# Global keys of batch 0 by short matmuls from the picked rows

## The chip, the cores and the metric

The kernel runs on one core of one Trainium2 chip. The metric is the time of the whole kernel on the device in microseconds (us). Measurements of one kernel are taken several times and the median is compared. TensorE is called PE in the profile, VectorE DVE, ScalarE ACT, GpSimd POOL and SyncE SP.

## The reference

Attention over 8 batches, 8 heads, 576 tokens and head size 64, followed by a two-layer feed-forward with squared ReLU (512 to 2048 to 512). Attention is local: a query sees the keys within 32 positions. Eight token indices, given at run time, are global: a global query sees every key, and every query sees the eight global keys.

```python
mask = np.abs(pos[:, None] - pos[None, :]) <= window
mask = mask | is_global[:, None] | is_global[None, :]
scores = np.where(mask, scores, -1000000000.0)
attn = np.exp(scores - max) / (sum + 1e-09)
x = (attn @ v) with heads side by side          # [4608, 512]
h = x @ w_in;  r = max(h, 0);  out = (r * r) @ w_out
```

## The kernel before, in words

**Layout.** A batch's 576 keys are cut into five tiles of 120 (the last 96). Each tile has 128 rows: rows 0 to 7 hold the eight global keys, the others the tile's own keys. The queries are laid out as 608 columns, four groups of 152: 144 tokens, then the eight global queries. A batch is worked in two halves of 304 columns. For each half a list of windows (WIN, or WIN2 without the two 8-column windows of the global queries) says which tile meets which columns. Since a window of columns often touches several tiles, a mask gives rows 0 to 7 a one only in the tile that owns a column, so that a global key counts once per query.

**Work on a head pair.** Heads go in pairs, four pairs per batch, numbered 0 to 3 in batch 0, 4 to 7 in batch 1 and so on. `scores` multiplies keys by queries into a PSUM bank pair ("sc" or "acc", by turns). `exps` is the exponential on ScalarE into `et`. `masked` multiplies by the mask on VectorE. `outputs` multiplies `et` by values for the numerators, and by ones for the denominators (in batches 0 and 1 by `one64` into a second bank, with the two heads of a pair on the two column halves of the array; L670). `finish_outputs` takes Ln and Exp of the negative on ScalarE for the reciprocal (L702, L703), sums the global queries' columns on VectorE (L709 in batch 0) and multiplies numerators by reciprocals into `xT` (L732), which is the input of the feed-forward. `global_outputs` normalizes the global queries. `scatter` (L751) then copies their eight columns to the run-time positions in `xT`, eight small copies on VectorE.

**Values of the global keys.** For batch 0 there is a one-hot matrix `oh` of the indices. `pick_values` multiplies it with the five value tiles (L449), VectorE casts the 8x512 result into `gv16` (L453), and `spread_values` (L457) copies it into rows 0 to 7 of each of the five value tiles, four copies on VectorE and one on ScalarE. Those rows had been set to zero by `clear_value_rows` (L441) at the start. For batch 1 the rows come from a fetch into `grow`, `gv16` is filled from there by ScalarE (L869) and spread in the same way. From batch 2 on, DMAs write the rows.

**Feed-forward.** It is cut into units. `mm1_half` (L543) is a pair of first-layer tiles for 256 tokens of chunk 0, eight units for the first 256 tokens and eight for the rest; `mm1` (L524) is one tile for 512 tokens of a later chunk; `mm2` (L587) is a quarter of the second layer for 128 tokens. The units wait in a Python list, and `take(n)` puts the next n into the instruction stream. Squares of the ReLU are on VectorE (L555), the ReLU mostly on ScalarE (L554).

**Order.** Nothing is scheduled automatically: every engine works through its instructions as written in the program. `SCHED` holds the counts: `g0`, `h0` to `h5`, `keep`, `b1` and `last` tell how many units are taken at which place, and the `w` entries how many filler matmuls of 512 columns on an idle tile `keep_warm` (L197) puts there; their results aren't used. In batch 0 the first halves of all four pairs are scored first (`half0`), then finished (`half0_out`, into "mm", "sc", "acc" and "mm" banks). `scatter(0, 0)` follows, then the first unit of chunk 0, then the second halves with units between. `scatter(0, 1)` comes ahead of the units for tokens from 256 on. There are three "mm" banks used in rotation and one "tr" bank.

**Queues.** Weights, batch 1's inputs and later values are fetched on GpSimd's queue in program order; three casts (L370) stand behind them, and then a one-element copy from `xT` (L909), which holds back the fetches for batch 2. Stores and transposing DMAs are on SP's queue.

Of the kernel before, what the change touches and what calls it, by code (L numbers as in the profile page):

```python
# [8 lines left out]
FP32 = mybir.dt.float32  # L9
# [3 lines left out]
AF = mybir.ActivationFunctionType  # L13
# [4 lines left out]
KT = 120  # L18
NT = 5
# [5 lines left out]
GTOK = 144  # L25
GRP = 152
NCOL = 608
BANKC = 304
# [11 lines left out]
)  # L40
W2 = 440
MB = (0, 456)
SCHED = dict(w8=2, w9=3, w5=3, w6=0, w7=4, wa=4, wb=3, wc=3, g0=1, w0=2, w1=4, w2=2, w3=2, w4=3, w=5, h0=0, h1=1, h4=1, h5=1, h2=1, h3=0, keep=1, b1=((3, 1, 3), (2, 1, 3), (2, 1, 3), (2, 1, 2)), last=((2, 1, 4), (3, 1, 4), (2, 1, 4), (2, 1, 7)))
ONES = 2.0**-7 * (1.0 + 15360.0 / 2**23)


# [1 line left out]
def kernel(  # L48
# [15 lines left out]
    P = 128  # L64
# [13 lines left out]
    def sbt(name, shape, dtype, bufs=1, tag=None):  # L78
        return sb.tile(shape, dtype, name=name, tag=(tag or name), bufs=bufs)
# [5 lines left out]
    def pst(tag, shape, dtype=FP32):  # L85
        return ps.tile(shape, dtype, name=tag, tag=tag, bufs=bufs_of[tag])
# [106 lines left out]
    def keep_warm(n):  # L193
        if n:
            w = pst("tr", [P, 512])
        for _ in range(n):
            nc.tensor.matmul(w, idle[:, 0:P], idle, start=True, stop=True)  # L197
# [245 lines left out]
            in_=idle[0:NG].rearrange("p (h d) -> p h d", d=D).unsqueeze(1).to_broadcast((NG, NT, H, D)),  # L443
        )

    def pick_values():
        gp = pst("mm", [P, 512])[0:NG]
        for x in range(NT):
            nc.tensor.matmul(  # L449
                gp.rearrange("p (h d) -> p h d", d=D), oh[:, x, :], vb[0][:, x, 0 : 2 * H : 2],  # L450
                start=(x == 0), stop=(x == NT - 1),
            )
        dve.tensor_copy(out=gv16, in_=gp.rearrange("p (h d) -> p h d", d=D))  # L453

    def spread_values(b, op, tiles=range(NT)):
        for x in tiles:
# [196 lines left out]
    lo, hi = slice(0, D), slice(D, P)  # L653
    PARTS = (((lo, 0, hi, 0), (hi, 1, lo, 1)), ((slice(0, P), 0, slice(0, P), 1),))

    def outputs(i, half, et, tag, wins, columns=False):
        b, hp = divmod(i, NHP)
        if tag == "mm":
            banks = [pst("mm", [P, 512]) for _ in range(2)]
        else:  # L660
            acc = pst(tag, [P, 2, 512])
            banks = [acc[:, x] for x in range(2)]
        vt = vb[b]
        vtf = vt.rearrange("p t x d -> p t (x d)")
        nw = len(wins[half])
        for n, (t, so, c0, w) in enumerate(wins[half] if columns else ()):
            o = c0 - half * BANKC
            for x in range(2):
                for e in range(2):
                    nc.tensor.matmul(  # L670
                        banks[x][D * e : D * e + D, o : o + w],
                        one64 if x else vt[:, t, 4 * hp + 2 * e], et[:, e, so : so + w],
                        start=(n == 0), stop=(n == nw - 1), skip_group_check=True,
                    )
        for e in () if columns else range(2):
            for n, (t, so, c0, w) in enumerate(wins[half]):
                o = c0 - half * BANKC
                vo = D * (4 * hp + e)
                nc.tensor.matmul(  # L679
                    banks[e][:, o : o + w], vtf[:, t, vo : vo + P], et[:, e, so : so + w],  # L680
                    start=(n == 0), stop=(n == nw - 1), skip_group_check=True,
                )
        return banks

    def global_outputs(b, gs, a, z, columns):
        gr = sbt("gr", [P, NHP, NG], FP32, bufs=2)
        if a == 0:
            gxs[b] = sbt("gx", [P, NHP, NG], FP16, bufs=2)
        for r, x, rs, xs in PARTS[columns]:
            dve.reciprocal(out=gr[r, a:z], in_=gs[rs, a:z, xs])  # L690
        for r, x, rs, xs in PARTS[columns]:
            dve.tensor_tensor(
                out=gxs[b][r, a:z], in0=gs[r, a:z, x], in1=gr[r, a:z], op=ALU.mult
            )

    def finish_outputs(i, half, acc, columns=False):
        b, hp = divmod(i, NHP)
        parts = PARTS[columns]
        av = [a[:, 0:BANKC].rearrange("p (k c) -> p k c", c=GRP) for a in acc]
        rec = sbt("rec", [P, 2, GTOK], FP32, bufs=4)  # L700
        for r, x, rs, xs in parts:
            act.activation(out=rec[r], in_=av[xs][rs, :, 0:GTOK], func=AF.Ln)  # L702
        act.activation(out=rec, in_=rec, func=AF.Exp, scale=-1.0)  # L703
        if b == 0:
            if half == 0:
                if hp == 0:
                    gsum[0] = sbt("gs", [P, NHP, 2, NG], FP32, bufs=2)
                for x in range(2):
                    dve.tensor_reduce(  # L709
                        out=gsum[0][:, hp, x], in_=av[x][:, :, GTOK:GRP].rearrange("p k g -> p g k"),  # L710
                        axis=AX.X, op=ALU.add,
                    )
                if hp >= NHP - 2:
                    a, z = (0, NHP - 1) if hp < NHP - 1 else (NHP - 1, NHP)
                    global_outputs(0, gsum[0], a, z, columns)
        else:
            if hp == 0 and half == 0:
                gsum[b] = sbt("gsh", [P, 2, NHP, 2, NG], FP32, bufs=2)
            for x in range(2):
                dve.tensor_reduce(  # L720
                    out=gsum[b][:, half, hp, x], in_=av[x][:, :, GTOK:GRP].rearrange("p k g -> p g k"),
                    axis=AX.X, op=ALU.add,
                )
            if hp == NHP - 1 and half == 1:
                gs = sbt("gs", [P, NHP, 2, NG], FP32, bufs=2)
                dve.tensor_tensor(out=gs, in0=gsum[b][:, 0], in1=gsum[b][:, 1], op=ALU.add)
                global_outputs(b, gs, 0, NHP, columns)
        x0 = b * S + half * HS
        if x0:
            x0 += XOFF  # L730
        for r, x, rs, xs in parts:
            dve.tensor_tensor(  # L732
                out=xT[r, hp, x0 : x0 + HS].rearrange("p (k x) -> p k x", k=2),
                in0=av[x][r, :, 0:GTOK], in1=rec[r], op=ALU.mult,
            )
# [46 lines left out]
    def half0(i):  # L782
        tag = pair_tag[i % 2]
        ets[i] = exps(0, scores(i, 0, tag, WIN), WIN)

    def half0_out(i, tag):
        acc = outputs(i, 0, ets[i], tag, WIN, columns=True)
        finish_outputs(i, 0, acc, columns=True)

    half0(0)  # L790
    cast_tokens(dve.tensor_copy, "k", 1)
    cast_tokens(dve.tensor_copy, "q", 1)
# [8 lines left out]
    tr_k(3, then=lambda: tr_q(3, act.copy))  # L801
    half0(2)
    keep_warm(SCHED["w6"])
    half0(3)
    columns()
    load_columns(0)
    pick_values()
    spread_values(0, dve.tensor_copy, range(0, 4))
    spread_values(0, act.copy, range(4, NT))
    masked(0, ets[2], WIN)  # L810
    masked(0, ets[3], WIN)
    for i in range(4):
        pool.dma_start(out=w_in[:, :, ts(i, 512)], in_=wv[:, :, ts(i, 512)])
    for i in range(0, NHP, 2):
# [5 lines left out]
    for j in range(4):  # L820
        pool.dma_start(out=w_out[:, ts(j, 4), :], in_=wo[:, ts(j, 4), :])
    next_in_place()
    keep_warm(SCHED["w7"])
    half0_out(0, "mm")
    half0_out(1, "sc")
    half0_out(2, "acc")
    half0_out(3, "mm")
    def half1(i):
        tag = pair_tag[i % 2]
        ets[i] = exps(1, scores(i, 1, tag, WIN2), WIN2)  # L830
# [141 lines left out]
```

The softmax here doesn't subtract the row's maximum and nothing guards it: scores larger than these inputs give would overflow.

## Time and profile before

| what | value |
|---|---|
| median of 8 runs | 326.55 us (326.22 to 327.94) |
| profiled execution, its own time | 326.69 us |
| its span in the profile | 324.9 us |
| TensorE busy | 316.5 us (97%) |
| VectorE, ScalarE, GpSimd busy | 225.8, 214.4, 110.9 us |
| first L543 matmul | at 24.46 us |
| first L543 matmul of the second half of chunk 0 | at 37.46 us |
| first L524 matmul | at 68.35 us |

The profile is one execution. Its span is 1.8 us shorter than that execution's time, since it leaves out what lies around the instructions. Fillers count as TensorE's busy time. A duration on TensorE holds the pipeline's latency, so matmuls in a row start closer together than they last; the rate is read from starts. In brackets stands the idle time ahead of a piece and who ended it.

### The profile page before, as it was taken

Reading aid. Unit: us, or ns where it says so; the run is one execution under the profiler, and the core shown is the slowest. Engines: PE = TensorE matmul, PEld = TensorE weight load, DVE = VectorE, ACT = ScalarE, POOL = GpSimd, SP = SyncE. Lnnn points to the kernel's source line nnn. Section 1 sums busy time; section 2 is a strip of 40 time slices with the busy share of each in tenths; the row PEclk is TensorE's granted clock in tenths of the full one; section 3 lists DMA queues with packets and bytes.
Section 4 is the critical chain, followed back from the end, with each engine's and each line's share of the span. In section 5 each row is a group of like instructions: output and inputs, shape, how many; then the busy total and the mean of one; then the engine's idle time right before and its main releaser. Section 6 shows DMA issues by size and latency. Waiting matters only on the chain.

```text
span 324.9 us, 6920 instructions
## 1 busy us (share of the span) xinstructions
PE 316.5 (97%) x2434; PEld 164.5 (51%) x2434; DVE 225.8 (70%) x674; ACT 214.4 (66%) x418; POOL 110.9 (34%) x148
## 2 busy tenths in 40 slices
PE   7989899999999999999999999999999999999995
PEld 3647674445554555555545554555445544444444
DVE  7596987688878885887598759875887685313411
ACT  6777885569855995499549954995499626404600
POOL 9934653649700960098108700780000000000000
DMA  8999999989994999499949994999710010021012
GB/s 187 177 205 190 168 188 169 169 140 121 153 119 142 82 146 153 138 88 154 135 149 77 149 142 142 86 147 108 157 46 0 34 67 31 2 78 51 2 55 74
DMA packets 148228, 37.53 MB, mean 116 GB/s; under 512 B 136170, under 2 KB 143714, under 8 KB 148194
## 3 DMA queue, kind: packets, MB, share of 16 engines
q0 software_dynamic: 105168, 17.93, 77.7%
q1 hardware_dynamic: 42880, 19.04, 30.3%
q8 instruction: 19, 0.31, 0.4%
q14 instruction: 15, 0.12, 0.1%
q10 hardware_dynamic: 146, 0.13, 0.1%
HBM read 37.30 MB, written 17.05 MB: 167 GB/s over the span
## 4 chain that ended last, share of the span: by engine, by line
PE 90%; DVE 5%; ACT 2%; issue 1%; DMA 0%
PE mm L587 29%; PE mm L524 26%; PE tr L524 9%; PE tr L587 7%; PE sc L679 3%; PE acc L679 3%; PE sc L627 3%; PE mm L543 2%; DVE xT L751 2%; PE acc L627 2%; PE tr L197 2%; PE sc L670 1%; DVE xT L732 1%; ACT rec L702 1%; PE acc L670 1%
## 5 line engine op out<-in xcount | busy, mean ns | idle before, releaser
L587 PE MATMUL mm<-w_out,gt 128*128 128x512 f16 x448 | 104.4, 379 | 0.0
L524 PE MATMUL mm<-xT,w_in 128*128 128x512 f16 x384 | 90.8, 379 | 0.6 <-DVE xT L751 0.6
L587 PEld LDWEIGHTS <-gt 128*128 128x128 f16 x560 | 52.4, 98 | 58.5
L524 PEld LDWEIGHTS <-w_in 128*128 128x128 f16 x512 | 47.5, 98 | 53.8 <-issue 0.9
L529 ACT ACTIVATE rl<-mm 128x512 f16<-128x512 f32 x96 | 54.3, 599 | 26.7 <-PE mm L524 26.7
L530 DVE TENSOR_TENSOR gt<-rl 128x512 f16<-128x512 f16 x128 | 51.1, 423 | 16.9 <-ACT rl L529 15.6
L636 ACT ACTIVATE et<-sc 128x880 f16<-128x880 f32 (+1 forms) x32 | 29.0, 907 | 43.9 <-PE sc L627 43.9
L643 DVE TENSOR_TENSOR et<-et,mask 128x880 f16<-128x880 f16 (+1 forms) x64 | 39.0, 615 | 24.0 <-ACT et L636 23.7
L113 POOL DMA_DIRECT2D vb<-in_v_dram x40 | 41.9, 1606 | 8.4 <-DMA w_in<-in_moe_w_in_dram 6.7
L524 PE MATMUL tr<-xT,w_in 128*128 128x512 f16 x128 | 32.9, 380 | 0.0
L564 DVE COPY ot<-mm 128x512 f32<-128x512 f32 (+1 forms) x29 | 19.7, 680 | 17.9 <-PE mm L587 16.2
L636 ACT ACTIVATE et<-acc 128x880 f16<-128x880 f32 (+1 forms) x32 | 29.1, 909 | 1.0 <-PE acc L627 1.0
L703 ACT ACTIVATE rec<-rec 128x288 f32<-128x288 f32 x64 | 28.3, 443 | 2.0
L732 DVE TENSOR_TENSOR xT<-sc,rec 64x288 f16<-64x288 f32 (+1 forms) x55 | 25.0, 455 | 6.5 <-ACT rec L703 6.1
L732 DVE TENSOR_TENSOR xT<-acc,rec 64x288 f16<-64x288 f32 (+1 forms) x55 | 25.0, 455 | 3.9 <-ACT rec L703 1.1
L404 POOL DMA_DIRECT2D scr_k<-in_k_dram x30 | 26.6, 1110 | 2.8 <-issue 2.8
L679 PEld LDWEIGHTS <-vb 128*128 128x128 f16 x288 | 21.3, 98 | 11.6
L930 POOL COPY pin<-gsh 1x1 f32<-1x1 f32 x5 | 0.9, 177 | 76.6 <-DVE gsh L720 76.6
L702 ACT ACTIVATE rec<-sc 64x288 f32<-64x288 f32 (+1 forms) x55 | 22.3, 406 | 6.2 <-PE sc L679 4.2
L404 POOL DMA_DIRECT2D scr_q<-in_q_dram x24 | 24.8, 1570 | 3.9 <-DMA w_out<-in_moe_w_out_dram 3.9
L587 PE MATMUL tr<-w_out,gt 128*128 128x512 f16 x112 | 25.3, 379 | 0.0
L702 ACT ACTIVATE rec<-acc 64x288 f32<-64x288 f32 (+1 forms) x55 | 22.2, 404 | 1.8 <-PE acc L670 1.0
(147 smaller groups left out, 306.7 us busy)
## 6 DMA issues: line engine op xcount, KB each, us to landing
out_dram<-ot SPq DMA_DIRECT2D x35, 256.0 KB
vb<-in_v_dram POOLq DMA_DIRECT2D x32, 120.0 KB, 10.8
scr_q<-in_q_dram POOLq DMA_DIRECT2D x24, 144.0 KB, 5.8
scr_k<-in_k_dram POOLq DMA_DIRECT2D x24, 120.0 KB, 4.4
w_in<-in_moe_w_in_dram POOLq DMA_DIRECT2D x4, 512.0 KB, 11.0
w_out<-in_moe_w_out_dram POOLq DMA_DIRECT2D x4, 512.0 KB, 12.4
natk<-in_k_dram POOLq DMA_DIRECT2D x3, 288.0 KB, 10.6
natq<-in_q_dram POOLq DMA_DIRECT2D x3, 288.0 KB, 11.1
```

The lines of the kernel that those rows point to most:

```text
L113: pool.dma_start(out=vb[b][NG : NG + KN[x], x, 2 * hs.start : 2 * hs.stop : 2], in_=v[b, hs, x * KT : x * KT + KN[x]].rearrange("h s d -> ...
L404: pool.dma_start(out=scr[(nm, b % 2)][x * pitch + off : x * pitch + off + hi - lo].rearrange("s (h d) -> s h d", d=D), in_=src[nm][b, :, l ...
L524: nc.tensor.matmul(ph, w_in[:, t, u * P : (u + 1) * P], xT[:, t, XOFF + c * TC : XOFF + (c + 1) * TC], start=(t == 0), stop=(t == NDM - 1),)
L529: nc.scalar.activation(out=rl, in_=ph, func=AF.Relu)
L530: nc.vector.tensor_tensor(out=gts[c][:, u, :], in0=rl, in1=rl, op=ALU.mult)
L587: nc.tensor.matmul(po, gts[c][:, f, m * P : (m + 1) * P], w_out[:, f, :], start=(f == 0), stop=(f == NFF - 1),)
L636: act.activation(out=et[:, :, 0:W], in_=sc[:, :, 0:W], func=AF.Exp, bias=0.0, scale=scale)
L643: dve.tensor_tensor(out=et[:, :, 0:W], in0=et[:, :, 0:W], in1=mask[:, MB[half] : MB[half] + W].unsqueeze(1).to_broadcast((P, 2, W)), op=AL ...
L679: nc.tensor.matmul(banks[e][:, o : o + w], vtf[:, t, vo : vo + P], et[:, e, so : so + w], start=(n == 0), stop=(n == nw - 1), skip_group_c ...
L702: act.activation(out=rec[r], in_=av[xs][rs, :, 0:GTOK], func=AF.Ln)
L703: act.activation(out=rec, in_=rec, func=AF.Exp, scale=-1.0)
L732: dve.tensor_tensor(out=xT[r, hp, x0 : x0 + HS].rearrange("p (k x) -> p k x", k=2), in0=av[x][r, :, 0:GTOK], in1=rec[r], op=ALU.mult,)
```

## The change

In batch 0 the picked rows are no longer copied into the value tiles, whose rows 0 to 7 stay zero. The outputs of a pair are first computed without the global keys' share of the numerators (their share of the denominators is in the ones matmul as before). Then `global_keys` adds it: for each window, the range of columns that its tile owns is multiplied with the eight rows of `gv16`, two matmuls with a contraction over 8 rows, one per head, accumulated into the same bank. There are three such ranges per pair and half, of 120, 128 and 48 columns in half 0 and 72, 128 and 96 in half 1, so 48 matmuls in all. `pick_values` is done in two halves of four heads. Pair 0's columns are computed in two pieces, the first ahead of pair 3's scores, into an "mm" and the "tr" bank; its reciprocals (`reciprocals`) can be issued ahead of the rest of `finish_outputs`; pairs 0 and 1 get their columns first and the global keys' share afterwards. `masked` of pair 2 moves ahead of the picking, that of pair 3 behind pair 1's columns. The global queries of all four pairs are normalized in one go. `spread_values` remains for batch 1. Counts in `SCHED` change with it.

```diff
-SCHED = dict(w8=2, w9=3, w5=3, w6=0, w7=4, wa=4, wb=3, wc=3, g0=1, ..., w=5, h0=0, h1=1, h4=1, h5=1, h2=1, h3=0, keep=1, ...)
+SCHED = dict(w8=2, w9=3, w5=3, w6=0, w7=0, wa=4, wb=2, wc=1, g0=1, ..., w=3, h0=1, h1=1, h4=1, h5=1, h2=0, h3=0, keep=2, ...)
...
-    def pick_values():
-        gp = pst("mm", [P, 512])[0:NG]
+    def pick_values(part):
+        gp = pst("mm", [P, 512])[0:NG, 0:256].rearrange("p (h d) -> p h d", d=D)
+        hs = slice(4 * part, 4 * part + 4)
         for x in range(NT):
             nc.tensor.matmul(
-                gp.rearrange("p (h d) -> p h d", d=D), oh[:, x, :], vb[0][:, x, 0 : 2 * H : 2],
+                gp, oh[:, x, :], vb[0][:, x, 8 * part : 8 * part + 8 : 2],
                 start=(x == 0), stop=(x == NT - 1),
             )
-        dve.tensor_copy(out=gv16, in_=gp.rearrange("p (h d) -> p h d", d=D))
+        dve.tensor_copy(out=gv16[:, hs], in_=gp)
...
+    def global_keys(i, half, et, banks, wins):
+        b, hp = divmod(i, NHP)
+        own = []
+        for t, so, c0, w in wins[half]:
+            cs = [
+                (max(KT * t + 8 * grp, GRP * grp, c0),
+                 min(KT * (t + 1) + 8 * grp, GRP * grp + GTOK, c0 + w))
+                for grp in range(4)
+            ]
+            cs = [c for c in cs if c[0] < c[1]]
+            if cs:
+                own.append((so - c0, cs[0][0], cs[-1][1]))
+        for n, (off, lo_, hi_) in enumerate(own):
+            for e in range(2):
+                nc.tensor.matmul(
+                    banks[0][D * e : D * e + D, lo_ - half * BANKC : hi_ - half * BANKC],
+                    gv16[:, 2 * hp + e], et[0:NG, e, off + lo_ : off + hi_],
+                    start=False, stop=(n == len(own) - 1), skip_group_check=True,
+                )
+
+    def outputs(i, half, et, tag, wins, columns=False):
+        b, hp = divmod(i, NHP)
+        banks = output_banks(tag)
+        if columns:
+            column_outputs(i, half, et, banks, wins, slice(None))
+            if b == 0:
+                global_keys(i, half, et, banks, wins)
+            return banks
...
-                if hp >= NHP - 2:
-                    a, z = (0, NHP - 1) if hp < NHP - 1 else (NHP - 1, NHP)
-                    global_outputs(0, gsum[0], a, z, columns)
+                if hp == NHP - 1:
+                    global_outputs(0, gsum[0], 0, NHP, columns)
...
     half0(2)
     keep_warm(SCHED["w6"])
+    first = [pst("mm", [P, 512]), pst("tr", [P, 512])]
+    column_outputs(0, 0, ets[0], first, WIN, slice(0, 3))
     half0(3)
     columns()
     load_columns(0)
-    pick_values()
-    spread_values(0, dve.tensor_copy, range(0, 4))
-    spread_values(0, act.copy, range(4, NT))
     masked(0, ets[2], WIN)
-    masked(0, ets[3], WIN)
+    pick_values(0)
+    pick_values(1)
+    column_outputs(0, 0, ets[0], first, WIN, slice(3, None))
...
     next_in_place()
-    keep_warm(SCHED["w7"])
-    half0_out(0, "mm")
-    half0_out(1, "sc")
-    half0_out(2, "acc")
-    half0_out(3, "mm")
+    reciprocals(0, first, True)
+    second = output_banks("sc")
+    column_outputs(1, 0, ets[1], second, WIN, slice(None))
+    masked(0, ets[3], WIN)
+    global_keys(0, 0, ets[0], first, WIN)
+    global_keys(1, 0, ets[1], second, WIN)
+    finish_outputs(0, 0, first, columns=True)
+    finish_outputs(1, 0, second, columns=True)
+    for i, tag in ((2, "acc"), (3, "mm")):
+        finish_outputs(i, 0, outputs(i, 0, ets[i], tag, WIN, columns=True), columns=True)
```

`column_outputs` is the loop of L666 to L674 of the kernel before, over a part of the windows; `output_banks` its choice of banks; `reciprocals` the three Ln and Exp lines.

## The prediction

> **What bounds the kernel now.** I read three views in this order: busy times and TensorE's waits, TensorE's timeline through the front, VectorE's timeline beside it.
>
> The page first, then who TensorE waited for (columns of the second: engine, line, releaser: total us, times, longest):
>
> ```profile
> span 324.9 us, 6920 instructions
> PE 316.5 (97%) x2434; PEld 164.5 (51%) x2434; DVE 225.8 (70%) x674; ACT 214.4 (66%) x418; POOL 110.9 (34%) x148
> ...
> PE mm L543 <- DVE xT L751: 2.1, 2, 1.2
> PE mm L524 <- DVE xT L751: 0.6, 1, 0.6
> ```
>
> TensorE is nearly always busy, but part of that is filler (keep_warm, L197). From 68.35 us to its last matmul it has no gap: the table by stretch gives 231.65 us busy of the 231.65 between 68.35 and 300. So the time can change in only two ways: first real work starts earlier, or work or waits before 68.35 change. All three late waits are on a scatter (L751). TensorE's timeline (start, duration, instructions, idle before):
>
> ```profile
> 14.59 0.40 PE L627 MATMUL acc<-qt,kt 64*128 64x160 f16 x10 [0.49 <-ACT qt L510]
> 14.92 1.24 PE L449 MATMUL mm<-vb,oh 128*8 128x512 f16 x5
> 16.10 1.04 PE L197 MATMUL tr<-idle 128*128 128x512 f16 x4
> 17.25 0.26 PE L670 MATMUL mm<-et,vb 128*64 128x160 f16 x2
> ...
> 24.46 1.03 PE L543 MATMUL mm<-xT,w_in 128*128 128x256 f16 x8 [1.24 <-DVE xT L751]
> ...
> 37.46 1.92 PE L543 MATMUL mm<-xT,w_in 128*128 128x256 f16 x16 [0.84 <-DVE xT L751]
> ```
>
> Outputs start at 17.25, only after the picked value rows were copied and spread; the first feed-forward matmul starts at 24.46. VectorE's timeline tells what lies between:
>
> ```profile
> 16.20 0.68 DVE L453 CAST gv<-mm 8x512 f16<-8x512 f32 x1 [1.76 <-PE mm L449]
> 16.91 0.89 DVE L457 COPY vb<-gv 8x512 f16<-8x512 f16 x4
> 17.73 1.16 DVE L643 TENSOR_TENSOR et<-et,mask 128x912 f16<-128x912 f16 x2
> 18.82 0.24 DVE L709 TENSOR_REDUCE gs<-mm 128x8 f32<-128x16 f32 x2
> ...
> 22.44 1.97 DVE L751 COPY xT<-gx 128x4 f16 x8
> ...
> 34.75 2.65 DVE L751 COPY xT<-gx 128x4 f16 x8
> ```
>
> VectorE idles 1.76 us, then runs almost without a gap to the scatter's end at 24.41. That chain sets 24.46.
>
> **What the skill says.** "TensorE: Matmul & The Clock Gate", section "Back-to-back issue gap", gives N/2.4 + 2.5 ns for a warm matmul, with a floor near 25 ns. The trace agrees: steps between pairs of L670 matmuls on the two column halves are 0.07 us at 160 columns and 0.03 us at 8. "TensorEngine Tiling (Array Packing)", "Key Properties", says that a change of tiling mode drains TensorE. The trace shows a little of it: scores (64-row tiles) of 440 columns take 0.30 us, where 440/2.4 is 0.18. "Advanced Engine Details and Errata", "VectorE Performance Modes", says GpSimd and two-port VectorE work block each other on a shared SBUF port. The scatter's copies do reach 0.53 us against 0.18 while GpSimd's three casts (L370) run from 34.81 to 36.5; the page is my reading of why.
>
> **The change, part by part.** All against the profiled span, 324.9 us, of a run of 326.69 us; the median, 326.55, is 0.14 lower, so I carry the difference over.
>
> *Spread removed (five L457 copies).* VectorE loses four (16.91 to 17.73, 0.82 us), ScalarE one of 0.62. Both stood before the outputs.
>
> *Early columns of pair 0.* Its first three windows now run before the scores of pair 3, in the 0.49 us gap before 14.59. They are six pair steps, 2×(0.07+0.085+0.04) = 0.39 us. Value tiles 0 to 2 landed by about 12.6 (issue at 4.0 to 6.1 plus 6.5 to 7.0 us). Hidden; uncovered it would cost 0.4.
>
> *Pick in two halves.* Ten matmuls of 256 columns stream what five of 512 did: end near 16.2 as before. VectorE now has something to do meanwhile: the mask of pair 2. Its exponential ends at 15.38, so the mask runs 15.40 to 15.95 (half of 17.73 to 18.82). Two casts of 8x256: 0.40 each, from 0.71 for 8x512 with a fixed part, to 16.75. The mask of pair 3: to 17.30. The new K=8 matmuls need the casts but follow pair 1's outputs, which end near 16.8, so pairs 0 and 1 are finished near 17.1. The reductions can start at 17.30, where they started at 18.82.
>
> *Denominators first.* They never need the picked rows, so ScalarE's Ln and Exp of pair 0 (0.42 and 0.44) run from about 16.3; at 0.775 us per pair ScalarE stays ahead of VectorE.
>
> *Reductions to scatter.* Before: 18.82 to 22.44, 3.62 us. Gone are a wait of 0.15 and one reciprocal with product (20.55 to 20.98, 0.43); the other pair becomes 32 wide (0.50 by the row at 65.39, instead of 0.32). 3.62 − 0.15 − 0.43 + 0.18 = 3.22. The scatter starts at 20.52; with its 2.02 to the first L543, that starts at 22.54 instead of 24.46: **1.92 us earlier**. The bank that pair 3's numerators reuse comes free after pair 0's product, near 17.95, just ahead of need. Fillers removed before this (w7 4, wb 1, w 2) filled idle time: worth nothing themselves. The remaining nine (wb 2, wa 4, w 3) leave a gap of about 1.3 us before L543, as the 1.24 before, so the clock should not fall.
>
> *K=8 matmuls in half 1.* Unseen before, both ends: at least the streaming, pairs of 72, 128 and 96 columns, 0.03+0.053+0.04 = 0.12 us per head pair; at most six in series at the 0.17 us that a lone 8-column matmul takes in the L479 rows, 1.0. They are pairs on two column halves like L670, so I take 0.12 + 0.05 for a drain = 0.17: four make +0.68. Half 0's four lie beside the VectorE chain.
>
> *Front of half 1.* From the first L543 to the first of tokens 288 on: 13.00 us before, 12.15 busy. Two fillers go (wc 3→1: 0.43), so busy is 12.15 − 0.43 + 0.68 = 12.40. An L543 unit takes the fillers' place (h0), h2 moves behind pair 3's outputs, and "keep" leaves one unit more. Waits: counting from the end of pair 3's scores, T (5.29 us after first L543 before; 5.29 + 0.98 − 0.43 + 0.34 = 6.18 now, so 28.72): ScalarE then has Ln and Exp of pair 2, two query copies (0.70), Ln and Exp of pair 3, done at T+3.97, the product at T+4.45. The scatter runs from 33.2; GpSimd's casts follow landed weights, so they stay at 34.8 and touch only its last copies: 2.0 to 2.3 us, not 2.65, ending near 35.4. TensorE waits some 0.5 for the score bank that the product frees, and is there at 35.4. Half 1 starts at about 35.45 instead of 37.46: **2.0 us earlier**.
>
> *Given back in batch 1's first pair.* Now only one half-1 unit, not two, lies between that start and the outputs that need the spread of batch 1 (unchanged, VectorE). VectorE from 35.4: one square 0.35, masks 1.05, spread 1.1, so its last tile is there near 37.9, while outputs reach it at about 37.5: **−0.35**.
>
> *End of batch 1.* One more unit kept means two L587 units instead of one (0.86 each) before the first L524, which waited 0.62 for scatter. The work is the same in all, the wait is covered: **+0.62**.
>
> Transfers: w_in's last quarter lands at 25.4, batch 1's keys and queries 0 and 1 at 27.0 and 28.5 (needed near 30), its values by 37.9 (tile 4 needed near 39), w_out's last at 47.8 (needed near 50). None is reached. GpSimd's next burst, batch 2's fetches (38.09), is held by the copy of a scattered value (L909) and so can start at most about 1 us earlier, behind the casts; it queues behind w_out and displaces nothing. On SP the unit shift puts the five fetches of batch 2's picked rows (L425, 4.1 us of issue at 60.16) ahead of the first store, not behind it; batch 2's values aren't read before 69.2, so both orders are in time: nothing.
>
> Sum: 2.0 − 0.35 + 0.62 = 2.27 us. Span 322.6; run 324.4; median 326.55 − 2.27 = **324.3**.
>
> **Rivals.**
> *Front gain is lost before half 1* (0.16). For it: the chain that ended last runs through VectorE from 34.26 to 43.98 and through ScalarE's Ln and Exp; both were 90% busy between 29.75 and 37.46, and casts and transfers there keep their own clock. If the second scatter ends at 36.5 and the spread delays outputs by 0.7: 0.96 − 0.7 + 0.62 = 0.9, 325.65 (325.2 to 326.5). Against: that stage loses work, gains none but K=8.
> *K=8 matmuls don't overlap* (0.10), the slower one. At 0.17 us each a head pair costs 1.02. Half 1: 4×0.85 more = +3.4; half 0: first sums later by 0.5, the last by about 1 more, +1.5. −2.27 + 4.9 = +2.6: 329.2. It decides at 0.17 + 2.27/4 = 0.74 us per head pair in half 1 alone. Against: 8-column L670 pairs step by 0.03. Another slower mishap I leave 0.04, a quarter of it within 0.2%.
> *Second scatter is clear of the casts and the spread is in time* (0.08): 2.0 + 0.5 + 0.62, 323.4.
>
> **How the numbers follow.** Main case 0.62, own range 323.6 to 325.2. About 0.65 us either way is all that a measurement tells from no change, so "faster" ends at 325.9: 0.62 + 0.08 + 0.10 of the first rival = 0.80; same 0.07, slower 0.13. The range 323.2 to 326.5 leaves out K=8 in series, half of the best case and a tail.
>
> **What would show it.** First L543 near 22.5, VectorE without the 1.76 us gap; scatter at 20.5; half-1 start near 35.4; no wait at L524; K=8 groups of about 0.17 us. Wrong if the reductions start at 18 or later, if outputs after the K=8 groups lag by over 0.3 us, or if TensorE shows new gaps between 28 and 40 us.

## The result, and the profile after

| | before | after |
|---|---|---|
| median | 326.53 us (326.09 to 327.94, 33 runs) | 330.63 us (327.65 to 331.88, 12 runs) |
| ratio to before, 95% interval | | 1.0104 [1.0086, 1.0122] |
| profiled execution and its span | 326.69, 324.9 us | 331.05, 329.3 us |

The change costs 4.1 us by the medians and 3.4 us by the ratio (0.0104 × 326.5), because the twelve runs lie far apart; what spreads them is told with e2_bridge. The prediction, 324.3 us with a range up to 326.5, was wrong in sign.

The page of the kernel after, its first lines and the row of the granted TensorE clock (40 slices of the span, 9 is full):

```profile
span 329.3 us, 7002 instructions
PE 320.4 (97%) x2478; PEld 168.0 (51%) x2478; DVE 226.1 (69%) x669; ACT 214.4 (65%) x417; POOL 110.4 (34%) x148
...
PEclk9957999999999999999999999999999999999999
```

The third and fourth slice (16 to 33 us) have lost clock. The page of the kernel before has no such row, but its fillers show the full rate there: four of 512 columns take 1.04 us at 16.10 and at 20.70, where four take 1.89 us at 24.91 after. TensorE's waits have a first entry that the kernel before did not have at all:

```profile
PE mm L450 <- issue: 2.3, 1, 2.3
```

"Issue" means that nothing the profile shows was being waited for: no semaphore, no engine, no data transfer. TensorE's timeline tells where (L450 are the picks, L449 before; L628 scores, L544 the first feed-forward unit):

```profile
14.47 0.40 PE L628 MATMUL acc<-qt,kt 64*128 64x160 f16 x10
17.17 1.60 PE L450 MATMUL mm<-vb,oh 128*8 128x256 f16 x10 [2.31 <-issue]
...
28.32 1.04 PE L544 MATMUL mm<-xT,w_in 128*128 128x256 f16 x8
...
40.02 2.79 PE L544 MATMUL mm<-xT,w_in 128*128 128x256 f16 x24
```

The early columns of pair 0 did go into the old gap ahead of 14.47, as intended. Then the picks, which before followed pair 3's scores at once (14.92), start 2.25 us later. VectorE's timeline shows the same from its side: the first cast waits 2.00 us, the sums begin at 20.46, and the scatter (L791) at 24.84, not 20.52 as predicted and not 22.44 as before.

```profile
17.91 0.41 DVE L454 CAST gv<-mm 8x256 f16<-8x256 f32 x1 [2.00 <-PE mm L450]
...
20.46 0.17 DVE L750 TENSOR_REDUCE gs<-mm 128x8 f32<-128x16 f32 x1 [0.69 <-PE mm L691]
...
24.84 2.04 DVE L791 COPY xT<-gx 128x4 f16 x8
...
39.70 1.65 DVE L791 COPY xT<-gx 128x4 f16 x8
```

The table by stretch of the same kernel. Its columns are stretch, length, busy time (and instructions) of TensorE, of its weight loads, of VectorE, ScalarE and GpSimd, then the granted clock, the mean share of the data-transfer engines, GB/s:

```profile
17.25:19.60 2.35, 2.35 (x30) 1.68 (x31) 1.20 (x3) 0.44 (x2) 0.93 (x1) 0.64 1.25 206
19.60:22.40 2.80, 2.80 (x58) 2.56 (x56) 1.50 (x7) 1.53 (x4) 0.92 (x1) 0.50 1.28 204
22.40:24.46 2.06, 2.06 (x28) 1.11 (x26) 1.53 (x8) 1.45 (x4) 0.86 (x1) 0.50 1.27 205
24.46:30.00 5.54, 5.54 (x46) 2.53 (x45) 2.89 (x11) 3.54 (x6) 2.51 (x4) 0.67 1.32 205
```

From 17.25 on TensorE is busy without a gap, but at half clock from 17.93 to 28.17, for 10.24 us (the granted clock of just this stretch is 0.50, and 1.00 on both sides). That makes the ledger of the front: predicted 22.54 for the first feed-forward matmul, found 28.32, 5.78 us later. Of these 17.17 − 14.92 = 2.25 are the late picks, and the way from the picks to the first unit took 28.32 − 17.17 = 11.15 us where the prediction had 22.54 − 14.92 = 7.62, 3.53 more, most of it the half clock: in e2_bridge below, at full clock, that way takes 25.97 − 17.64 = 8.33 with all of pair 0's columns in it. Against the kernel before the first unit is 3.86 us late (24.46), pair 8's scores with the one unit more that is kept for behind them 69.67 + 0.86 − 66.13 = 4.40, the span 4.4. So all that counts happens ahead of 70 us, and most of it ahead of 28.

### The profile page after: what moved, and what is told of

Same layout as the page of the kernel before. It is cut to its first block, busy times and chain, and to the rows that moved or that the text cites. A ratio compares the mean times of both kernels' runs of the same rounds, so it can differ in the third digit from the quotient of the medians.

```text
span 329.3 us, 7002 instructions
## 1 busy us (share of the span) xinstructions
PE 320.4 (97%) x2478; PEld 168.0 (51%) x2478; DVE 226.1 (69%) x669; ACT 214.4 (65%) x417; POOL 110.4 (34%) x148
## 3 DMA queue, kind: packets, MB, share of 16 engines
q0 software_dynamic: 105168, 17.93, 77.4%
## 4 chain that ended last, share of the span: by engine, by line
PE 91%; DVE 6%; ACT 1%; issue 1%
PE mm L588 28%; PE mm L525 25%; PE tr L525 9%; PE tr L588 7%; PE sc L712 3%; PE mm L544 3%; PE acc L712 3%; PE sc L628 3%; PE tr L197 2%; PE acc L628 2%; PE acc L670 1%; DVE xT L791 1%; DVE et L644 1%; PE sc L670 1%; PE mm L471 1%
## 5 line engine op out<-in xcount | busy, mean ns | idle before, releaser
L113 POOL DMA_DIRECT2D vb<-in_v_dram x40 | 41.1, 1578 | 9.1 <-DMA w_in<-in_moe_w_in_dram 7.4
```

The lines of the kernel that those rows point to most:

```text
L113: pool.dma_start(out=vb[b][NG : NG + KN[x], x, 2 * hs.start : 2 * hs.stop : 2], in_=v[b, hs, x * KT : x * KT + KN[x]].rearrange("h s d -> ...
```

## The experiments

Times of one batch come from one chip; ratios are to the runs of the kernel before on that chip, whose median was 327.08 us for e1 to e4, 326.56 for e5 to e8, 327.15 for e9 to e12 and 326.57 for e13 to e15.

### What makes the picks late: e1_shift

The data-transfer view of the kernel after, in the quarter microsecond from 14.75 (packets, MB, share of 16 engines), shows a transfer of another kind among the data, on a queue of instructions. It has 19 packets of 16 KB in the whole run:

```profile
q0 software_dynamic: 46, 0.05, 111.8%
q8 instruction: 1, 0.02, 24.1%
```

The Trainium skill, "Runtime: NRT & Kernel Launch", section "Instruction fetch mechanics", says that an engine's instructions are refilled in 16 KiB blocks of 256 by a queue of its own, and that a crossing is "mostly hidden". The count fits TensorE's queue (2,478 matmuls and as many weight loads, divided by 256, are 19.4). The theory: the crossing at the picks is not hidden, because the block is late. It is then tied to a place in the instruction stream.

```diff
+    pad = pst("tr", [P, 512])
+    for _ in range(10):
+        nc.tensor.matmul(pad[:, 0:8], idle[:, 0:P], idle[:, 0:8], start=True, stop=True)
     gb = indices()
```

(after, with ten 8-column matmuls near the start)

> The changed kernel with ten more tiny matmuls (8 columns of zeros) at its start, so that everything after them on TensorE stands 20 instructions later in its stream. Theory 1, the gap of 2.3 us is TensorE waiting for its next block of instructions: the gap stays about as long but moves to an instruction that stands 20 earlier, so it lies within or ahead of pair 3's scores (L628 acc) and no longer between them and the picks (L450). Theory 2, the gap is a wait of the picking for its operands (value tiles, bank): it stays in front of the picks. Theory 3, the K=8 matmuls or the missing fillers cause the loss: gap unchanged in place.

Measured: 329.13 us in one run (before there 327.08), span 327.2, clock 0.995 (half clock for 3.41 us, from 16.74). TensorE's timeline:

```profile
16.96 0.58 PE L628 MATMUL acc<-qt,kt 64*128 64x160 f16 x10 [2.26 <-DVE et L644]
17.47 2.29 PE L450 MATMUL mm<-vb,oh 128*8 128x256 f16 x10
```

The gap has moved to the instructions ahead, pair 3's scores, with the same length; the picks follow at once. (The name behind the arrow is that of the last semaphore and not of a work that was late.) Pair 3's scores are ten matmuls and ten weight loads, so the stop moved by exactly the twenty instructions that were put ahead of it; nothing that the stopped instruction needs had changed.

The other profiles say the same. Up to the stop the profile counts 222 matmuls and 223 weight loads in the kernel after, in e1_shift and in e4_hold, and 223 and 223 in e3, e9, e13 and e15. In the kernel before 219 and 219 stand ahead of 17.25, so the same place is some seven instructions into pair 0's outputs. And where TensorE stands waiting at this place, its next instruction starts a like time after the end of the packet: 1.39 us in the kernel after (15.78 to 17.17), 1.39 in e1_shift, 1.40 in e3_pickfirst, 1.41 in e4_hold, and between 1.23 and 1.50 in seven more.

### Is the block late because of the data: e4_hold

```diff
     column_outputs(0, 0, ets[0], first, WIN, slice(3, None))
+    pool.tensor_copy(out=pin[0:1], in_=ets[2][0:1, 0, 0:1])
     for i in range(4):
         pool.dma_start(out=w_in[:, :, ts(i, 512)], in_=wv[:, :, ts(i, 512)])
```

(after, with the fetches of the weights and of batch 1 held back until pair 2's mask)

> The changed kernel with the fetch of w_in held back on GpSimd until pair 2's mask is done (about 15.9 us), so that few transfers run between 15 and 16 us. Theory 1 with the block's transfer late because data transfers fill the DMA engines: the gap ahead of the picks shrinks to under 1 us. If the block's arrival doesn't depend on the other transfers the gap stays at 2.3 us. The weights land later: the time itself can go either way, 324 to 331 us.

Measured: 331.69 us (330.82 to 331.90, 4 runs), ratio 1.0139 [1.0122, 1.0156]. It is slower, outside the range of the expectation, since batch 1's tokens now come late, and the clock falls to half again behind these waits (for 3.41 us, from 34.21). For the question only the front counts: the packet of the instruction block starts at 13.0 us instead of 14.8, and

```profile
15.36 1.25 PE L450 MATMUL mm<-vb,oh 128*8 128x256 f16 x10 [0.34 <-PE acc L628]
...
33.87 0.45 PE L471 MATMUL mm<-identity,natq 96*64 96x96 f16 x12 [1.01 <-DMA natq<-in_q_dram]
```

With fewer data transfers ahead of the block the gap is 0.34 us instead of 2.31. (When the block was asked for, the profile doesn't show, so what kept it in the kernel after isn't seen directly.) In the kernel before the block was as late (its packet at 14.86 us), but the crossing fell into pair 0's first outputs, which waited for the spread values until 17.25, behind fillers. The wait that the change removed had covered another of nearly the same length.

### The clock behind the gap: e2_bridge

```diff
-    first = [pst("mm", [P, 512]), pst("tr", [P, 512])]
-    column_outputs(0, 0, ets[0], first, WIN, slice(0, 3))
     half0(3)
+    keep_warm(12)
     columns()
...
-    column_outputs(0, 0, ets[0], first, WIN, slice(3, None))
+    first = [pst("mm", [P, 512]), pst("tr", [P, 512])]
+    column_outputs(0, 0, ets[0], first, WIN, slice(None))
```

> Early columns of pair 0 moved behind the picks, and twelve fillers of 512 columns (2.6 us, as many instructions) put in their place behind pair 3's scores. The picks still start near 17.2 us under theory 1, but TensorE is busy until then. If the fall of the clock is what turned the gap into the loss: clock 1.0 throughout, first L543 near 24.5 us instead of 28.3, and a time near 326.0 us (within 1 us of the kernel before). If the loss is the K=8 matmuls' own cost, the time stays near 330 us.

Measured: 328.66 us (328.54 to 328.69, 4 runs), ratio 1.0043 [1.0026, 1.0060]. The picks start half a microsecond later still than in the kernel after (second row below), but TensorE came to them busy, and the stretch from 17 us keeps the full clock (second fence, 1.00):

```profile
14.94 2.76 PE L197 MATMUL tr<-idle 128*128 128x512 f16 x12
17.64 1.25 PE L450 MATMUL mm<-vb,oh 128*8 128x256 f16 x10
```

```profile
17.00:20.00 3.00, 3.00 (x56) 2.04 (x55) 1.36 (x3) 0.43 (x2) 0.93 (x1) 1.00 1.26 205
```

The first unit starts at 25.97, 2.35 us earlier than after. The clock came as expected, the time (near 326.0) did not: 1.6 us above the kernel before are left. By the ratios the half clock costs 0.0061 × 326.5 = 2.0 us. That compares two chips, and e2's profile holds 0.72 us at pair 8 that the profile after does not (told below).

The twelve runs of the kernel after put it higher. They lie in steps: 327.65 and 327.81 us with a mean granted clock of 1.000, 328.66 and 328.98 with 0.995, 330.01 with 0.990, 330.5 to 331.1 with 0.983 or 0.984, 331.88 with 0.979. The full-clock runs are 2.9 us below the median of 330.63, and only 1.2 above the kernel before. No trace of those two was kept, so whether their gap was as long isn't known. The half clock is then 2 to 3 of the 4.1 us.

### The gap gone too: e3_pickfirst, e9_again, e15_third

```diff
-    first = [pst("mm", [P, 512]), pst("tr", [P, 512])]
-    column_outputs(0, 0, ets[0], first, WIN, slice(0, 3))
     half0(3)
...
     pick_values(1)
-    column_outputs(0, 0, ets[0], first, WIN, slice(3, None))
+    keep_warm(2)
+    first = [pst("mm", [P, 512]), pst("tr", [P, 512])]
+    column_outputs(0, 0, ets[0], first, WIN, slice(None))
```

(after, with all of pair 0's columns behind the picks: 24 instructions fewer ahead of them)

> Early columns of pair 0 moved behind the picks, two fillers behind the picks. 24 fewer instructions stand ahead of the picks. Theory 1: the picks run at about 15 us and the gap follows them (some 0.5 us left to 17.2), the clock stays at 1.0, the scatter starts near 21.4 us and the time is 324.8 to 325.8 us, faster than before. Theory 2: the picks still wait until about 17.2 us and the time is 328 us or more.

> The kernel with the picks ahead of pair 0's columns, unchanged, run again beside the three that follow. Theory of the instruction supply on ScalarE: the late exponential of pair 8 follows from the place of an instruction block in ScalarE's stream, so it starts some 2 us after its scores again, TensorE waits about 1.4 us at pair 8's outputs, and the ratio is 1.003 as before. Rival: the late exponential belonged to the chip of that batch and not to the kernel; then it is prompt here, the wait at pair 8's outputs is 0.2 us, and the ratio falls to about 1.000 (1.2 us less), which would leave nothing over for the K=8 groups' 1.1 us.

> The kernel with the picks ahead of pair 0's columns, unchanged, as the anchor of this batch: ratio 1.0025 (1.002 to 1.003) as in its two earlier runs, exponential of pair 8 1 to 2 us after its scores.

Measured, on three chips: 328.30 us, ratio 1.0032 [1.0023, 1.0041]; 327.88, 1.0022 [1.0015, 1.0030]; 327.34, 1.0021 [1.0009, 1.0032]. Theory 1's order came, its time (324.8 to 325.8 us) did not. The crossing now falls into pair 0's columns, and little of the wait is left to see (timeline of e3_pickfirst):

```profile
14.90 1.25 PE L450 MATMUL mm<-vb,oh 128*8 128x256 f16 x10
...
17.22 0.26 PE L670 MATMUL mm<-et,vb 128*64 128x160 f16 x1 [0.34 <-issue]
```

The clock is 0.998 to 1.000. By the medians 1.2, 0.7 and 0.8 us of the loss are left, so the gap and the half clock behind it are 2.9 to 3.4 of the 4.1 us. By the ratios 0.7 to 1.0 us are left, and they are 2.4 to 2.7 of 3.4.

### What the K=8 groups cost: e7_nokeys1, e13_nokeys2, e14_fill, e10_twice, e12_k128

Timeline of the kernel after, one group with the columns' last matmul ahead of it and what follows:

```profile
29.63 0.23 PE L670 MATMUL sc<-et,one 128*64 128x136 f16 x2
29.79 0.32 PE L691 MATMUL sc<-et,gv 8*64 8x72 f16 x6
30.04 0.39 PE L197 MATMUL tr<-idle 128*128 128x512 f16 x1
```

From start to start a group is 0.25 us, where the prediction had 0.17; four are 1.0 us. e7 and e13 are e3 without the groups in half 1, that is, without the global keys' share of the numerators of those tokens:

```diff
-            if b == 0:
+            if b == 0 and half == 0:
                 global_keys(i, half, et, banks, wins)
```

> e3 without the K=8 matmuls of half 1 (the global keys' share of the numerators is left out there, so part of the computation is missing). The profiles show 0.25 us for each of these four groups where 0.17 was predicted. If they lie on the path, the time falls by 1.0 us (0.3%) against e3; if VectorE or ScalarE sets the pace between 24 and 37 us it falls by less than 0.4 us.

> As e15_third, but without the K=8 matmuls of half 1 (the global keys' share of the numerators of those tokens is left out), on the same chip as the two others. If the groups cost their 0.25 us each, it is 1.0 us below e15_third, a ratio of 1.000 against 1.0025, and exponential and outputs of pair 8 follow without a wait above 0.3 us. Rival: the difference between the earlier two batches belonged to the chips; then the two ratios agree within 0.001, and the wait at pair 8's outputs is 0.8 us or more in both.

Measured: e7 326.66 us, ratio 0.9997 [0.9985, 1.0009]; e13 326.69, ratio 1.0002 [0.9993, 1.0011]. On one chip with e15_third (1.0021) the groups are worth 0.0019, 0.6 us (0.1 to 1.1 by the two intervals). So the term of +0.68 held in the total; the single group is longer, and the effect of four on the end smaller than their length. One place where the difference goes: without the groups the outputs of batch 1's first pair wait 0.70 and 0.16 us for the spread values (38.69 and 39.41 in e13), with them 0.36 (e15).

e14_fill puts a filler of 0.22 us in the place of each group (`elif b == 0: keep_warm(1)`).

> As e13_nokeys2 with one full-width filler matmul (0.22 us at full clock) in the place of each K=8 group of half 1. If what the groups cost is TensorE's time in that place, this one is 0.9 us above e13_nokeys2, close to e15_third. Rival: the groups cost through what they make wait (the late exponential of pair 8), not through their own time; then this one stays within 0.3 us of e13_nokeys2.

Measured: 327.45 us, ratio 1.0026 [1.0017, 1.0035], 0.8 us above e13, as the first theory had it. But it isn't a clean copy: the filler shares the "tr" bank, and one of the four waited for it (timeline):

```profile
33.99 0.39 PE L197 MATMUL tr<-idle 128*128 128x512 f16 x1 [0.81 <-DVE kt L501]
```

So e13 and e15 show that the groups cost time at the end; whether they do it through TensorE's own time, e14 can't tell, because how much of its 0.8 us is the fillers' and how much that wait is open.

e10_twice issues each group of half 1 twice (a second `global_keys` call if `half`); e12_k128 takes 128 rows in place of 8 there (`gv16` with 128 rows, zeroed, and `et[0:128]`).

> As e9_again with every group of K=8 matmuls of half 1 issued twice (the global keys' numerators of the tokens of half 1 are counted twice). Theory: a group costs 0.25 us of TensorE on the path, so four more cost 1.0 us, a ratio 0.003 above e9_again's. Rival 1, part of the 0.25 us is the change from the columns' tile to the K=8 tile, paid once for a group however long: then four doubled groups add 4 x 0.12 = 0.5 us, 0.0015. Rival 2, nothing shows because the wait ahead of half 1's units takes it up: less than 0.2 us.

> As e9_again with the extra matmuls of half 1 over all 128 rows (the picked rows in a tile whose other rows are zero) in place of K=8: same columns, same count. Theory: the 0.25 us of a group is the streaming of its columns, 296 columns in 0.12 us, and a change of the row tile from 128 to 8 rows of about 0.13 us; without the change a group costs 0.12 to 0.15 us and the kernel is 0.4 to 0.5 us below e9_again. Rival: the cost lies in short matmuls as such; then a group stays at 0.25 us and the time is e9_again's within 0.2 us.

Measured beside e9_again's 1.0022: e10 327.66 us, 1.0019 [1.0010, 1.0027]; e12 327.76, 1.0023 [1.0012, 1.0034]. In time neither theory came; the rivals that expected no difference did. The timelines say more. Around the same place, without a group (e13_nokeys2), with 8 rows (e15_third) and with 128 rows (e12_k128):

```profile
25.36 0.23 PE L670 MATMUL sc<-et,one 128*64 128x136 f16 x2
25.52 0.39 PE L197 MATMUL tr<-idle 128*128 128x512 f16 x1
```

```profile
25.00 0.23 PE L670 MATMUL sc<-et,one 128*64 128x136 f16 x2
25.16 0.32 PE L691 MATMUL sc<-et,gv 8*64 8x72 f16 x6
25.41 0.39 PE L197 MATMUL tr<-idle 128*128 128x512 f16 x1
```

```profile
25.06 0.23 PE L670 MATMUL sc<-et,one 128*64 128x136 f16 x2
25.12 0.30 PE L692 MATMUL sc<-et,gv 128*64 128x72 f16 x6
25.35 0.39 PE L197 MATMUL tr<-idle 128*128 128x512 f16 x1
```

From the columns' last matmul to what follows the group it is 0.16 us without a group, 0.41 with 8 rows and 0.29 with 128. A group thus adds 0.25 us with 8 rows and 0.13 with 128. Over the four places the sums are 1.05 and 0.52 us, and issuing the groups twice (e10) adds 0.13 us for each second pass. The theory of e12 holds for a group's length: half of the 0.25 us is the streaming of the columns, half comes with the tile of 8 rows and goes with it. (The step from the group's own start to the next, 0.25 with 8 rows and mostly 0.23 with 128, hides this, because with 128 rows the group starts 0.06 us after the columns instead of 0.16.)

That e12's 0.5 us don't show in the time fits the wait told next: pair 8's outputs start at 69.34 in e12 as in e9, behind a wait of 1.51 us instead of 0.80. For e10 this wasn't tried apart; its profiled execution ran some 1.5 us late from the front on.

### A late exponential in batch 2: e5_actpad and e11_pad2

In e1 to e4 TensorE waited 0.7 to 1.5 us at the outputs of pair 8, because ScalarE began that pair's exponential about 2 us after its scores (start of the scores at 66.02 in e3_pickfirst, ScalarE's row below). The kernels before and after show no such thing.

```profile
68.33 0.90 ACT L637 ACTIVATE et<-sc 128x880 f16<-128x880 f32 x1 [3.15 <-remote]
```

The guess was an instruction block of ScalarE's. e5 is e3 with twelve tiny ScalarE copies behind `clear_value_rows()`; e11 has them three at a time behind the exponentials of batch 1's pairs:

```diff
     clear_value_rows()
+    padt = sbt("padt", [1, 8], FP16)
+    for _ in range(12):
+        act.copy(out=padt, in_=idle[0:1, 0:8])
```

> e3 with twelve tiny copies (8 elements) more at the start of ScalarE's stream, where it idles. In e3 the exponential of pair 8 (the first of batch 2) began at 68.33 us though its scores were there at 66.4, and TensorE then waited 1.45 us for its mask. Theory A, ScalarE waits there for its next block of instructions: twelve places earlier in its program the border falls elsewhere, the exponential starts within 0.3 us of its scores, TensorE's wait falls below 0.6 us and the time is about 1 us (0.3%) below e3's. Theory B, the exponential is late for another reason (order of units, a transfer): wait and time as in e3.

> As e9_again with twelve tiny ScalarE copies, three after the exponentials of each pair of batch 1, where ScalarE waits for TensorE anyway. Theory of the instruction supply on ScalarE: if e9_again has the late exponential of pair 8, it is prompt here (starts 0.3 us after its scores), the wait at pair 8's outputs falls from 1.4 to 0.2 us, and the kernel is about 1 us below e9_again. Rival: the late exponential has another cause; then it stays late, and the time is e9_again's or up to 0.5 us more.

Measured: e5 329.70 us (4 runs), ratio 1.0101 [1.0070, 1.0133]; e11 328.66 (4 runs), 1.0042 [1.0025, 1.0059]. In e5 the exponential is prompt, but the copies delay the first query cast, and TensorE stands still until 8.34 us and loses clock again (0.72 between 8 and 14 us):

```profile
8.34 0.43 PE L467 MATMUL mm<-identity,nat0q 96*128 96x96 f16 x6 [1.74 <-ACT nat0q L434]
```

In e11 it is as late as ever (start 68.64, scores at 66.64), with the same shift of ScalarE's stream. The guess fell. What goes with it is the chip: it is late in all eight profiles of the two batches in which the kernel before took 327.1 us, and prompt in all seven of the two in which it took 326.6, the unchanged kernel of e3, e9 and e15 among them, late in the first two and, against its expectation, prompt in e15 (TensorE's wait at pair 8's outputs in e9_again and in e15_third):

```profile
69.34 0.62 PE L712 MATMUL sc<-et,vb 128*128 128x160 f16 x6 [0.80 <-DVE et L644]
```

```profile
68.26 0.62 PE L712 MATMUL sc<-et,vb 128*128 128x160 f16 x6 [0.23 <-DVE et L644]
```

It has no part in the 4.1 us: the profile after has 0.23 us in that place.

### The unit that covers the scatter: e6_keep2

```diff
-SCHED = dict(..., keep=1, ...)
+SCHED = dict(..., keep=2, ...)
```

(the kernel before, this count alone)

> The kernel before with keep=2 alone, so that one unit more is left for later. By the prediction's step for the end of batch 1 the wait of 0.62 us ahead of the first L524 goes and the time falls by about 0.6 us (0.2%). Rival: the outputs of pair 8, which now come right behind the two L587 units, wait instead for their mask behind the scatter, and the time stays or rises by up to 0.8 us.

Measured: 326.80 us (12 runs), ratio 1.0007 [0.9998, 1.0015]. The wait of 0.62 ahead of L524 is gone, but so is the unit's place in half 1, where waits stand that the kernel before did not have, as there is one at pair 8:

```profile
37.51 1.05 PE L543 MATMUL mm<-xT,w_in 128*128 128x256 f16 x8 [0.50 <-ACT rl L554]
40.11 0.23 PE L670 MATMUL sc<-et,vb 128*64 128x88 f16 x2 [0.36 <-DVE vb L457]
...
68.47 0.62 PE L679 MATMUL sc<-et,vb 128*128 128x160 f16 x6 [0.23 <-DVE et L643]
```

With 0.20 at the scores of batch 1's first pair (34.78), 1.29 us come where 0.62 and the 0.84 ahead of half 1 go. A unit kept for later is a unit taken from where it covered something.

### A version without K=8 in half 1: e8_spread1

e3 with the global queries' chain first (denominators ahead of numerators, the groups of pair 0 right behind its columns), ScalarE spreading the picked rows into tiles 2 to 4 between the halves so that half 1 needs no groups, keep=1, wc=0:

```diff
-            if b == 0:
+            if b == 0 and half == 0:
                 global_keys(i, half, et, banks, wins)
...
     scatter(0, 0)
-    globals_in_place("k")
-    globals_in_place("q")
+    spread_values(0, act.copy, range(2, NT))
```

> Picks first as in e3; in half 0 the denominators are computed ahead of the numerators and pair 0's K=8 matmuls directly behind its columns; for half 1 ScalarE spreads the picked rows into value tiles 2 to 4 (three copies of 0.56 us) and no K=8 matmuls are used; keep=1 as before, h0=1, h2=0, no filler between the first two outputs of half 1. If instruction supply, K=8 groups in half 1 and the extra unit kept are what e3 lost: first L543 near 23.4 us, second half near 36.6, time 0.7 to 1.0 us below the kernel before. If ScalarE's copies delay half 1: within 0.3 us of the kernel before or slower.

Measured: 327.06 us (326.55 to 327.98, 20 runs), ratio 1.0013 [1.0006, 1.0019]. By the ratios 0.3 to 0.6 us better than e3, not better than the kernel before. The spread, off VectorE, comes back as ScalarE's time (1.64 us at 24.86), ahead of its ReLUs and reciprocals, and TensorE waits at three places that the kernel before doesn't have: 0.38 at 31.05, 0.49 at 34.08 and 0.35 at 41.32. (The profiled execution, 327.88 us, ran some 1.7 us late from the front on.) No version here beats the kernel before.

## Why the prediction was wrong, point by point

**"End near 16.2 as before" (the picks): the step that failed.** They end at 18.8, because a block of TensorE's instructions isn't there: 2.31 us of waiting in a place where the prediction had none. The step moved the picks' neighbours, and it counted instructions' durations only. The packet on the instruction queue at 14.86 us could be read before, and that the outputs behind the spread wait began at 17.25; which instruction the packet brings became plain only from the stop. e3_pickfirst, with no spread to wait for, goes on behind the block at 17.22. The prediction took all of that wait to be the spread's. It removed one of two causes that ended together.

**"Fillers removed ... worth nothing", "so the clock should not fall": failed with it.** Four fillers (w7) stood from 16.10 to 17.14 in the very stretch that became the gap. Behind the gap of 2.31 us the clock was half for 10.24 us in the profiled execution, which is 2 us at the end by e2_bridge and 2.9 by the full-clock runs of the kernel after.

**Reductions to scatter, "1.92 us earlier": right in its start, too short in its length.** Where the gap is small, in e4_hold, the reductions start at 17.63; the prediction with that gap's 0.34 added is 17.64. From there to the scatter it takes 3.55 us, and 3.54 in e15_third, where the prediction had 3.22 and the kernel before 3.62. ScalarE does not stay ahead, as "Denominators first" had it: VectorE waits for its reciprocals twice (e15_third).

```profile
18.44 0.17 DVE L750 TENSOR_REDUCE gs<-mm 128x8 f32<-128x16 f32 x1 [1.36 <-PE mm L691]
...
19.50 0.46 DVE L772 TENSOR_TENSOR xT<-sc,rec 128x288 f16<-128x288 f32 x1 [0.22 <-ACT rec L736]
...
20.34 0.46 DVE L772 TENSOR_TENSOR xT<-acc,rec 128x288 f16<-128x288 f32 x1 [0.22 <-ACT rec L736]
...
21.98 1.66 DVE L791 COPY xT<-gx 128x4 f16 x8
```

So of the 1.92 us some 1.6 would have been left without the gap (an estimate from e4_hold: 1.92 less 0.33); no run had the order of the change and no gap. In e15_third, with pair 0's columns behind the picks, the first unit starts at 23.69, 0.77 earlier than before.

**K=8, +0.68: near in the sum.** 0.6 us by e15 against e13, loosely (0.1 to 1.1). A group is 0.25 us, not 0.17: its streaming was right (0.12, measured 0.13), its 0.05 for a drain is 0.12 by e12. The slower rival that named it (groups in series, 0.74 us per head pair or more) didn't come.

**Front of half 1, "2.0 us earlier": failed.** In e15_third half 1 starts at 37.29 instead of 37.46. From the first unit to there it takes 13.60 us, before 13.00, predicted 12.91: mainly the groups' extra 0.3 and a wait of 0.50 for the second scatter, which took 2.68 us there and 1.65 in the profile after, where no cast of GpSimd's ran beside it. That part of the first rival's reasoning, and the prediction's reading of the casts, stand.

**Batch 1's first pair, −0.35: right.** Waits of 0.25 (after) and 0.36 us (e15) for the spread tile.

**End of batch 1, +0.62: failed.** e6_keep2 did it alone and gained nothing (−0.2 us, interval −0.5 to +0.1).

With most of the gap, the half clock and the groups of half 1 gone (e7, e13) the ratio is 0.9997 and 1.0002: what is left of the change is worth nothing within 0.4 us, where the prediction had 2.27 + 0.68 = 2.95 us. Some 0.4 of that goes with pair 0's columns behind the picks in these runs, and 0.33 with the chain above. The rest is lost on the way: in e13 half 1 starts 1.16 us earlier than before (36.30), pair 8's scores, with the unit kept back counted, only 0.20 (65.07 + 0.86 against 66.13). Between them stand the 0.86 us of waits for the spread values, and the unit kept back was worth as much where it came from (e6_keep2). The case that came, a new wait in the place of the one removed, in a resource that no step looked at, was none of the rivals; it was in the "other mishap" of 0.04.

## What to carry to other kernels

When a wait is to be removed, ask what else was due at the moment when it ended, and look at the instruction queues among the transfers too: a wait that ends just when an instruction block lands may be hiding that block. Take fillers out only after the new order's gaps are known, since a gap of 2.3 us cost more through the clock behind it (2 to 3 us) than through itself. The block boundary stood at a fixed count of TensorE's instructions, whatever they were, so the same edit with twenty instructions more or less can give another result.

## What was not expected of the hardware

- An instruction block cost 2.31 us in full view. Its packet starts at 14.8 us and takes 0.96 us, its first instruction runs at 17.17, while data transfers on the same engines ask for 112 to 128% of their time. With fewer transfers ahead (e4_hold) it comes 1.8 us earlier and costs 0.34. From the packet's end to that instruction it is 1.23 to 1.50 us in eleven traces. The later blocks of that profile (20.8, 30.4, 40.0 us and on) cost nothing visible.
- The clock went to half behind a gap of 2.31 us. "TensorE: Matmul & The Clock Gate", section "What's actually happening", puts an idle window of about 3.4 us before that. The half clock lasted 10.24 us there and 3.41 in e1_shift, whose gap was 2.26, and in 2 of the 12 runs of the kernel after it never fell; so its length depends on more than the gap's.
- Six short matmuls (72, 128 and 96 columns, two heads) add 0.25 us behind outputs of 128 rows when they have 8 rows, 0.13 when they have 128, and 0.13 for a second pass. The change to the short tile and back costs as much as the columns.
- The late exponential: in the trace of e3_pickfirst the last matmuls of pair 8's two score halves start at 66.18 and 66.44 us, and the change of TensorE's semaphore for them is recorded at 68.31 and 68.39; ScalarE starts at 68.33. In e7_nokeys1 the same changes follow at 66.04 and 66.30 on starts at 65.82 and 66.07. Between 66.2 and 68.3 no semaphore at all changes for stretches of 0.59, 0.67 and 0.57 us. What holds them is open.
